# An opening list ordered anew, and U's first lower part taken by VectorE instead of a second sum on TensorE

## The chip, the cores and the metric

The kernel runs on one core of a Trainium2 chip. The metric is the device time of one execution in microseconds (us). Before the change three runs took 706.29, 706.46 and 708.8 us; the median is 706.46 us. The chance that a text gives to "the same" means within 0.5% of it.

## The reference, cut to what matters

An attention over 32 learned memory slots, 8 batches of 8 heads, feeds a gated feed-forward layer over 4608 tokens. All is float32.

```python
a = softmax(phi)                                    # over the 576 positions, per memory slot
k_m, v_m = a.T @ k, a.T @ v                         # 32 slots per head
attn = softmax(q @ k_m.T / 8) @ v_m                 # 576 x 64 per head
x = attn heads side by side                         # 4608 x 512
out = (1 / (1 + exp(-(x @ w_gate))) * (x @ w_val)) @ w_out      # d_ff 1536
```

## The kernel before, in words

The product attn @ v_m @ [w_gate, w_val] is never made by way of x. For a batch b and a slice f of 128 of the 1536 columns the kernel makes U = v_m @ [w_gate, w_val] first (32 slots of 8 heads = 256 rows), and then G = U^T @ attn^T. A float32 product of this weight would take TensorE several passes, so each operand is split in an upper part that is rounded to the one-pass type fp32r, and a lower part, which is the rest; G and O are then the sum of three one-pass products (upper by upper, upper by lower, lower by upper). The pieces before that (T, K, t, S, U) are plain float32.

The first 20 of the 32 steps (b, f) of the first half, some 180 us of the span, are written out by hand in one list, OPENING. Each entry is traced behind the entry before it on TensorE, VectorE, ScalarE and GpSimd (`queued`, `step`), so on every one of these engines the instructions stand in the list's order; loads stand in the list's order on SyncE's queue (`move`). After the list a loop, ordered by the scheduler, goes through the rest. The names in the list (b is the batch, c one of two cuts of the 576 positions, 256 and 320 wide):

| entry | engine | what |
|---|---|---|
| phi, kvt, kvm, q, gate, out, more | SyncE | loads; gate and out fetch words of the weights, 8 bytes a number |
| amax, aexp, Z | VectorE, ScalarE, VectorE | softmax over phi |
| T, A | TensorE, ScalarE | transpose of it (two of 512 columns, one of the tails), copy out of PSUM |
| K, B, t, V | TensorE, ScalarE, TensorE, ScalarE | k_m and v_m, scaled, transposed, kept as kT (V b 0) and vT (V b 1) |
| S, mx, ms, ex, nz, nm | TensorE, then VectorE but ex on ScalarE | scores and softmax; tp (batch 0) or tr and tn turn them |
| hi, lo | ScalarE, VectorE | upper and lower part of attn^T |
| sz, bt / ws, wb, wh, wl | ScalarE, VectorE / ScalarE and VectorE | words of w_gate, w_val / w_out made into float32 and split |
| U, uh, ul | TensorE, ScalarE, VectorE | U for two f at a time, its upper and lower part |
| G, sg, gm, gh, gl | TensorE, ScalarE, VectorE, ScalarE, VectorE | gate and value, sigmoid, product, its two parts |
| O, E, row | TensorE, ScalarE, SyncE | times w_out, copy out, store |
| W n | TensorE | n fillers: matmuls whose result nobody reads, to keep the engine running |

PSUM has eight banks; four rotate under the name pu_t, three of the acc banks join them until the first O.

One pair, (b 0, f 0 and 1), is in BY_PE: its lower part is not subtracted. `um 0 0` multiplies the upper part by a tile `minus` (the identity times -1) and adds U's eight products a second time in the same banks; what is left in PSUM is U minus its upper part, and ScalarE copies it (`u_rest`, L773). All other pairs go through `u_lo`, whose subtraction is `rest` (L246). `copy` (L230) goes to ScalarE or, with act=False, to VectorE.

Of the kernel before, what the change touches and what calls it, by code (L numbers as in the profile page):

```python
# [78 lines left out]
q 1 0; ex 0 0; mx 0 1; U 0 0; q 1 1; A 1 0; out 1; A 1 2; ms 0 1; uh 0 0; nz 0 0; ex 0 1; W 10;
um 0 0; nm 0 0; sz 3; nz 0 1; tp 0 0; nm 0 1; hi 0 0; W 7; ul 0 0; lo 0 0; K 1 0; tp 0 1; hi 0 1;  # L80
wb 0; G 0 0 0; sz 2; kvm 2 0; lo 0 1; amax 2; G 0 0 1; wh 0; aexp 2; G 0 1 0; bt 3; wl 0; K 1 1;
bt 2; sg 0 0 0; G 0 1 1; B 1; kvt 2; kvm 2 1; gm 0 0 0; sg 0 0 1; out 2; gh 0 0 0; gm 0 0 1; out 3;
sg 0 1 0; t 1; gl 0 0 0; T 2 1; gm 0 1 0; V 1 0; Z 2; T 2 2; sg 0 1 1; S 1 0; V 1 1; gm 0 1 1;
A 2 1; tr 1 0; S 1 1; gh 0 0 1; U 0 2; tr 1 1; A 2 2; T 2 0; uh 0 2; mx 1; U 1 0; A 2 0; ul 0 2;
gh 0 1 0; K 2 0; uh 1 0; ms 1; ws 1; ul 1 0; K 2 1; gl 0 0 1; ex 1; O 0 0 0; gl 0 1 0; wb 1; nz 1;
wh 1; more 0; G 0 2 1; kvt 3; B 2; phi 3; kvm 3 0; wl 1; O 0 0 1; nm 1; G 0 2 0; sg 0 2 0;
gh 0 1 1; G 0 3 0; sg 0 2 1; gm 0 2 0; ws 2; tn 1; O 0 1 0; gh 0 2 0; hi 1; G 0 3 1; gm 0 2 1;
gl 0 2 0; gl 0 1 1; gh 0 2 1; wb 2; sg 0 3 0; lo 1; t 2; sg 0 3 1; O 0 1 1; wh 2; gm 0 3 0; sz 4;
q 2 0; wl 2; q 2 1; G 1 0 0; gl 0 2 1; keep 0; ws 3; gm 0 3 1; amax 3; O 0 2 0; G 1 0 1; gh 0 3 0;
sg 1 0 0; gl 0 3 0; V 2 0; wb 3; gh 0 3 1; V 2 1; gm 1 0 0; more 1; sg 1 0 1; O 0 2 1; wh 3;  # L90
gm 1 0 1; wl 3; S 2 0; S 2 1; tr 2 0; aexp 3; O 0 3 0; tr 2 1; gl 0 3 1; mx 2; U 1 2; gh 1 0 0;
E 0 3 0 0; T 3 2; E 0 3 0 1; row 0 3 0; O 0 3 1; gl 1 0 0; uh 1 2; ms 2; row 0 3 1; G 1 1 0;
gh 1 0 1; ul 1 2; ex 2; O 1 0 0; gl 1 0 1; nz 2; G 1 1 1; sg 1 1 0; A 3 2; gm 1 1 0; E 0 3 1 0;
gh 1 1 0; T 3 0; row 0 3 2; sg 1 1 1; nm 2; G 1 2 0; kvm 3 1; E 0 3 1 1; keep 1; gm 1 1 1; O 1 0 1;
sg 1 2 0; tn 2; gh 1 1 1; G 1 2 1; gm 1 2 0; A 3 0; T 3 1; sg 1 2 1; G 1 3 0; gl 1 1 0; gh 1 2 0;
phi 4; gm 1 2 1; A 3 1; bt 4; hi 2; O 1 1 0; more 2; sz 5; lo 2; K 3 0; gl 1 1 1; q 3 0; gl 1 2 0;
U 2 0; q 3 1; sg 1 3 0; keep 2; gm 1 3 0; K 3 1; Z 3; O 1 1 1; B 3; amax 4; uh 2 0; G 1 3 1;
gh 1 2 1; ul 2 0; gh 1 3 0; O 1 2 0; bt 5; sg 1 3 1; sz 6; gm 1 3 1; G 2 0 0; more 3; gl 1 2 1;
row 0 3 3; gl 1 3 0; t 3; sg 2 0 0; G 2 0 1; V 3 0; gm 2 0 0; gh 1 3 1; V 3 1; gh 2 0 0; S 3 0;
sg 2 0 1; gm 2 0 1; O 1 2 1; tr 3 0; aexp 4; S 3 1; U 2 2; tr 3 1; gh 2 0 1; O 1 3 0; mx 3; uh 2 2;  # L100
G 2 1 0; E 1 3 0 0; ul 2 2; E 1 3 0 1; gl 1 3 1; O 1 3 1; row 1 3 1; ms 3; ws 4; G 2 1 1; gl 2 0 0;
ex 3; gl 2 0 1; nz 3; O 2 0 0; sg 2 1 0; E 1 3 1 0; G 2 2 0; gm 2 1 0; E 1 3 1 1; gh 2 1 0;
sg 2 1 1; O 2 0 1; sg 2 2 0; gm 2 1 1; row 1 3 0; gm 2 2 0; gh 2 1 1; G 2 2 1; gh 2 2 0; gl 2 2 0;
gl 2 1 0; bt 6; U 3 0; sg 2 2 1; gl 2 1 1; more 4; O 2 1 0; uh 3 0; row 1 3 2; gm 2 2 1; kvt 4;
nm 3; G 2 3 0; ul 3 0; O 2 1 1; sg 2 3 0; tn 3; gh 2 2 1; G 2 3 1; gm 2 3 0; hi 3; O 2 2 0; lo 3;
sg 2 3 1; again 0; sz 7; row 1 3 3; gl 2 2 1; G 3 0 0; gm 2 3 1; O 2 2 1; gh 2 3 0; sg 3 0 0;
gh 2 3 1; gm 3 0 0; G 3 0 1; wb 4; gl 2 3 0; more 5; O 2 3 0; sg 3 0 1; wh 4; gm 3 0 1; gl 2 3 1;
G 3 1 0; Z 4; E 2 3 0 0; wl 4; E 2 3 0 1; row 2 3 0; gh 3 0 0; T 4 1; row 2 3 1; sg 3 1 0;
gl 3 0 0; U 3 2; A 4 1; gm 3 1 0; G 3 1 1; uh 3 2; gh 3 0 1; ul 3 2; O 2 3 1; sg 3 1 1; gl 3 0 1;
bt 7; G 3 2 0; E 2 3 1 0; sg 3 2 0; E 2 3 1 1; gm 3 1 1; more 6; O 3 0 0; gh 3 1 0; G 3 2 1; ws 5;  # L110
O 3 0 1; gl 3 1 0; gm 3 2 0; sg 3 2 1; wb 5; gm 3 2 1; U 0 4; wh 5; row 2 3 2; keep 3; G 3 3 0;
uh 0 4; kvm 4 1; row 2 3 3; gh 3 1 1; ul 0 4; more 7; O 3 1 0; gh 3 2 0; gl 3 2 0; G 3 3 1;
gl 3 1 1; wl 5; sg 3 3 0; ws 6; O 3 1 1; sg 3 3 1; gh 3 2 1; gm 3 3 1; G 0 4 0; gm 3 3 0; gl 3 2 1;
O 3 2 0; sg 0 4 0; gh 3 3 0; gm 0 4 0; gl 3 3 0; wb 6; U 0 6; O 3 2 1; uh 0 6; wh 6; ul 0 6;
G 0 4 1; gh 3 3 1; O 3 3 0; sg 0 4 1; gh 0 4 0; gm 0 4 1; gl 3 3 1; E 3 3 0 0; E 3 3 0 1; gh 0 4 1;
G 0 5 0; gl 0 4 0; row 3 3 0; O 3 3 1; sg 0 5 0; row 3 3 1; gm 0 5 0; again 1; gl 0 4 1; gh 0 5 0;
wl 6; G 0 5 1; O 0 4 0; sg 0 5 1; E 3 3 1 0; gm 0 5 1; E 3 3 1 1; row 3 3 2; G 0 6 0; kvm 4 0;
more 8; row 3 3 3; O 0 4 1; sg 0 6 0; ws 7; gm 0 6 0; gl 0 5 0; G 0 6 1; gh 0 5 1; fetch 0 0; wb 7;
gh 0 6 0; gl 0 5 1; O 0 5 0; sg 0 6 1; gm 0 6 1; gl 0 6 0; G 0 7 0; sg 0 7 0; wh 7; gh 0 6 1; wl 7;
T 4 2; O 0 6 0; gm 0 7 0; gl 0 6 1; gh 0 7 0; A 4 2; gl 0 7 0; sz 8; fetch 0 1; T 4 0; O 0 7 0;  # L120
# [1482 lines left out]
```

## Time and profile before

| what | us |
|---|---|
| runs | 706.29, 706.46, 708.8 |
| the profiled execution's own time | 706.82 |
| its span, first to last instruction | 705.0 |
| TensorE busy | 697.7 |
| VectorE busy | 520.7 |
| ScalarE busy | 403.0 |
| GpSimd busy | 97.2 |

The span is what the rows of the profile add up to; 1.8 us of the execution lie outside it. A busy TensorE says little by itself, since fillers count as busy and a matmul's end is modelled: what it could have done without is found by looking at which matmuls stand in a stretch and how far apart they start.

### The profile page before, as it was taken

What the parts mean: (1) busy time and instruction counts of PE and PEld (TensorE: products, weight loads), DVE (VectorE), ACT (ScalarE), POOL (GpSimd) and SP (SyncE); (2) the same over time, 40 slices, a digit from 0 to 9 for tenths busy, and PEclk for the clock granted to TensorE, in tenths of its full rate; (3) what the DMA queues carried; (4) which work ended last, traced back from release to release, by engine and by line L of the source; (5) the groups of instructions that cost most, each with busy time, mean ns of one, the idle gap of its engine ahead of it and who ended that gap; (6) DMA issues with size and microseconds to landing.
All of it is one profiled execution on the core that took longest, in us unless ns stands there. A gap on an engine that the chain in (4) does not pass through costs nothing.

```text
span 705.0 us, 15881 instructions
## 1 busy us (share of the span) xinstructions
PE 697.7 (99%) x6295; PEld 621.3 (88%) x6295; DVE 520.7 (74%) x1086; ACT 403.0 (57%) x915; POOL 97.2 (14%) x135
## 2 busy tenths in 40 slices
...
GB/s 359 413 275 339 253 196 170 232 136 250 280 253 265 276 183 135 133 351 244 164 113 182 148 357 206 292 271 43 284 137 164 227 108 276 77 295 56 238 111 105
DMA packets 52298, 151.49 MB, mean 215 GB/s; under 512 B 5888, under 2 KB 24320, under 8 KB 50176
## 3 DMA queue, kind: packets, MB, share of 16 engines
...
## 4 chain that ended last, share of the span: by engine, by line
PE 98%; DMA 1%; DVE 1%; ACT 0%; issue 0%; DVEq 0%; POOL 0%; POOLq 0%; SPq 0%
PE pu_t L256 59%; PE acc L256 38%; DMA ph<-in_phiT_dram 1%; DVE row L1291 0%; ACT ph L224 0%; DVE nmx L430 0%; DVEq L1599 0%; DVE x L1291 0%; POOL ident masks.py:199 0%; POOL ident masks.py:197 0%; POOLq masks.py:199 0%; SPq L242 0%; DVEq L1291 0%; POOLq L1593 0%
## 5 line engine op out<-in xcount | busy, mean ns | idle before, releaser
L256 PE MATMUL pu_t<-at_hi,u_hi 128*128 128x256 f32 (+1 forms) x760 | 224.5, 295 | 0.0
L256 PE MATMUL pu_t<-at_hi,u_lo 128*128 128x256 f32 (+1 forms) x760 | 222.6, 293 | 0.0
L256 PE MATMUL pu_t<-at_lo,u_hi 128*128 128x256 f32 (+1 forms) x760 | 222.6, 293 | 0.0
L256 PEld LDWEIGHTS pu_t<-at_hi,u_hi 128*128 128x128 f32 x760 | 142.8, 188 | 4.3 <-issue 1.4
L256 PEld LDWEIGHTS pu_t<-at_lo,u_hi 128*128 128x128 f32 x760 | 142.7, 188 | 2.0
L256 PEld LDWEIGHTS pu_t<-at_hi,u_lo 128*128 128x128 f32 x760 | 142.6, 188 | 0.0
L246 DVE TENSOR_TENSOR g_lo<-x,g_hi 128x128 fp32r<-128x128 f32 (+2 forms) x193 | 88.5, 464 | 15.0 <-ACT g_hi L1103 13.8
L224 ACT ACTIVATE x<-pu_t 128x320 f32<-128x320 f32 (+1 forms) x128 | 52.2, 410 | 81.8 <-PE pu_t L256 81.0
L1053 DVE TENSOR_TENSOR x<-pu_t,x 128x320 f32<-128x320 f32 (+1 forms) x128 | 58.1, 455 | 47.2 <-ACT x L224 29.1
L256 PE MATMUL acc<-wo_hi,g 128*128 128x512 f32 x256 | 91.1, 400 | 0.0
L256 PE MATMUL acc<-wo_hi,g_hi 128*128 128x256 f32 x276 | 78.3, 284 | 0.0
L256 PE MATMUL acc<-wo_lo,g_hi 128*128 128x256 f32 x276 | 76.9, 278 | 0.0
L256 PE MATMUL acc<-wo_hi,g_lo 128*128 128x256 f32 x276 | 76.8, 278 | 0.0
L246 DVE TENSOR_TENSOR u_lo<-pu_t,u_hi 128x512 fp32r<-128x512 f32 x92 | 58.3, 682 | 13.9 <-ACT u_hi L230 13.9
L242 POOL DMA_DIRECT2D out_dram<-row x48 | 42.4, 966 | 145.1 <-DVE row L1197 132.4
L256 PEld LDWEIGHTS acc<-wo_hi,g 128*128 128x128 f32 x256 | 48.0, 188 | 15.3 <-issue 5.8
L256 PEld LDWEIGHTS acc<-wo_hi,g_hi 128*128 128x128 f32 x276 | 51.8, 188 | 10.1 <-issue 9.2
L256 PE MATMUL acc<-ring,g_hi 128*128 128x256 f32 x332 | 60.2, 281 | 0.0
L256 PEld LDWEIGHTS acc<-ring,g_hi 128*128 128x128 f32 x332 | 50.5, 188 | 9.2 <-issue 6.7
L1103 ACT CAST g_hi<-x 128x512 fp32r<-128x512 f32 x63 | 39.1, 620 | 30.9 <-DVE x L1101 30.9
L230 ACT CAST u_hi<-pu_t 128x512 fp32r<-128x512 f32 x92 | 49.0, 590 | 12.3 <-PE pu_t L256 7.8
L256 PEld LDWEIGHTS acc<-wo_hi,g_lo 128*128 128x128 f32 x276 | 51.8, 188 | 0.0
...
## 6 DMA issues: line engine op xcount, KB each, us to landing
...
words<-in_wgv_dram SPq DMA_DIRECT2D x5, 1023.6 KB, 7.5
...
```

Of the source, the lines that this page charges most:

```text
L224: last_act[0] = nc.scalar.activation(*args, **kw)
L230: (nc.scalar.copy if act != swapped[0] else nc.vector.tensor_copy)(to, x)
L242: last_move[queue] = queues[queue].dma_start(dst, src, **how)
L246: return nc.vector.tensor_tensor(lo, x, hi.bitcast(F32), op=ALU.subtract)
L256: last_pe[0] = do(*args, **kw)
L1053: last_prod[0] = nc.vector.tensor_tensor(x[:, :n], val, x[:, :n], op=ALU.mult)
L1103: nc.scalar.copy(gh[:, 2:6], x[:, 1:5])
```

## The change

It takes BY_PE, `u_minus`, `u_rest` and the tile `minus` away, so that `ul 0 0` is a VectorE subtraction like all others. The list holds the same entries otherwise, in another order, with fillers W of other number and at other places, and 44 entries bear a ' behind their name: their copies go to the other engine (22 gh', ten A', four V', three hi' and three uh' go from ScalarE to VectorE, two wh' the other way). `swapped` already was in the kernel and no entry used it.

```diff
-BY_PE = [(0, 0)]
 OPENING = """
-phi 0; gate 0; kvm 0 0; kvt 0; kvm 0 1; amax 0; aexp 0; W 24; T 0 0; T 0 2; T 0 1; A 0 2; A 0 0;
...
+W 4; W 4; W 6; W 2; phi 0; W 4; W 1; amax 0; aexp 0; T 0 1; Z 0; T 0 0; A' 0 0; W 2; W 5; T 0 2; kvt 0;
+kvm 0 0; kvm 0 1; A' 0 2; K 0 0; A 0 1; K 0 1; B 0; t 0; W 2; W 1; W 4; V 0 0; V' 0 1; q 0 0; q 0 1;
...
 """
...
-    def u_minus(b, fs):
-
-        pb, hi = loaded[b, "u", fs[0]], U[b, fs[0]][0]
-        for r in range(2):
-            matmul(pb[r], minus, hi[:, r, : len(fs)], start=True, stop=False)
-        u_sum(b, fs, pb, False)
-
-    def u_rest(b, fs):
-        pb, nf = loaded.pop((b, "u", fs[0])), len(fs)
-        hi, lo = U[b, fs[0]]
-        for r in range(2):
-            last_u[0] = nc.scalar.copy(lo[:, r, :nf], pb[r])
...
-    minus = pools["conv"].tile([P, P], F32R, name="minus", bufs=1)
-    nc.scalar.activation(minus, ident, AF.Copy, scale=-1.0)
...
-        "ul": lambda b, f: (u_rest if (b, f) in BY_PE else u_lo)(*pair(b, f)),
+        "ul": lambda b, f: u_lo(*pair(b, f)),
```

The fillers: before, 24 stand ahead of the list and 76 in it, all ahead of the first G; now 24 and 111, of which 104 ahead of the first G.

SyncE's queue, the first loads of the kernel before. wg_106 and wg_105 are the words of w_gate and w_val for f 0 and 1 (gate 0, gate 1).

```order
L242 DMA ph<-in_phiT_dram 128x1152
L242 DMA wg_106<-in_wgv_dram 128x8189
L242 DMA kvm_150<-in_kvm_dram 128x2048
L242 DMA kvt<-in_kvt_dram 128x512
L242 DMA kvm_154<-in_kvm_dram 128x2048
L242 DMA q<-in_qT_dram 128x1024
L242 DMA ph<-in_phiT_dram 128x1152
L242 DMA wg_105<-in_wgv_dram 128x8189
```

The same queue now; at_hi takes the third phi.

```order
L240 DMA ph<-in_phiT_dram 128x1152
L240 DMA kvt<-in_kvt_dram 128x512
L240 DMA kvm_200<-in_kvm_dram 128x2048
L240 DMA kvm_202<-in_kvm_dram 128x2048
L240 DMA q<-in_qT_dram 128x1024 x2
L240 DMA q<-in_qT_dram 128x256
L240 DMA ph<-in_phiT_dram 128x1152
L240 DMA wg_106<-in_wgv_dram 128x8189
L240 DMA at_hi<-in_phiT_dram 128x1152
L240 DMA wg_105<-in_wgv_dram 128x8189
```

The loads of batch 0 moved ahead of the weights' words, and the third phi moved ahead of the second of them.

ScalarE around U's first parts, before: acc_383 and acc_384 are U's two banks, e the scores of batch 0.

```order
L224 ACTIVATE e<-e 128x512
L230 COPY left<-pu_t 128x512
L230 COPY tails<-pu_t 64x128 x2
L230 CAST u_hi<-acc_383 128x512
L230 CAST u_hi<-acc_384 128x512
L224 ACTIVATE e<-e 128x640
L273 ACTIVATE wg_102<-wg_103,over 128x1024
L274 ACTIVATE wg_102<-wg_102,under 128x1024
L230 CAST at_hi<-acc_437 128x2x256
L773 CAST u_lo<-acc_383 128x512
L773 CAST u_lo<-acc_384 128x512
```

ScalarE now, from the second exponential of the scores (ex 0 1) to the first sigmoid; the words of f 0 (two pairs of 128x512) stand right ahead of it. wg_101 is the tile of f 0 and 1, acc_450 and acc_451 are U's banks, wo_raw takes words of w_out (ws 0).

```order
L222 ACTIVATE e<-e 128x640
L271 ACTIVATE wg_101<-wg_105,over 128x1024
L272 ACTIVATE wg_101<-wg_101,under 128x1024
L228 COPY left<-pu_t 128x512
L222 ACTIVATE at_hi,z<-at_hi,nmx 128x576 x2
L271 ACTIVATE wo_raw<-words,over 128x512
L272 ACTIVATE wo_raw<-wo_raw,under 128x512
L228 CAST at_hi<-acc_423 128x2x256
L228 CAST u_hi<-acc_450 128x512
L228 CAST u_hi<-acc_451 128x512
L222 ACT_TABLE_LOAD
L222 ACTIVATE sg<-acc_506 128x256
```

The words of f 0 and 1 moved behind the first exponential, the third softmax over phi (two exponentials of 128x576) and the words ws 0 moved to between the second one and U's upper part, and the two casts of U's lower part are gone.

VectorE at the same place, before: the first lower part of attn^T and what follows it.

```order
L246 TENSOR_TENSOR at_lo<-acc_437,at_hi 128x2x256
L356 SCALAR_TENSOR_TENSOR wo_raw<-words,wo_raw 128x512
L246 TENSOR_TENSOR at_lo<-pu_t,at_hi 128x2x256
L246 TENSOR_TENSOR at_lo<-pu_t,at_hi 128x2x64
L430 TENSOR_REDUCE nmx<-at_hi 128x2
L230 CAST wo_hi<-wo_raw 128x512
```

VectorE now.

```order
L244 TENSOR_TENSOR at_lo<-acc_423,at_hi 128x2x256
L244 TENSOR_TENSOR u_lo<-acc_450,u_hi 128x512
L244 TENSOR_TENSOR u_lo<-acc_451,u_hi 128x512
L228 CAST at_hi<-pu_t 128x2x256
L228 CAST at_hi<-pu_t 128x2x64
L354 SCALAR_TENSOR_TENSOR wo_raw<-words,wo_raw 128x512
L244 TENSOR_TENSOR at_lo<-pu_t,at_hi 128x2x256
L244 TENSOR_TENSOR at_lo<-pu_t,at_hi 128x2x64
```

U's two subtractions and the upper part of the second cut were added to VectorE ahead of the first G.

## Rows read from the trace of the kernel before

**Rows 1.** The page's head and its busy times.
```profile
span 705.0 us, 15881 instructions
PE 697.7 (99%) x6295; PEld 621.3 (88%) x6295; DVE 520.7 (74%) x1086; ACT 403.0 (57%) x915; POOL 97.2 (14%) x135
```

**Rows 2.** Stretches: length, then PE, PEld, DVE, ACT, POOL busy, clock, DMA share, GB/s.
```profile
0.00:20.00 20.00, 17.51 (x190) 14.10 (x191) 6.16 (x15) 11.94 (x25) 0.70 (x6) 1.00 0.92 364
20.00:80.00 60.00, 59.97 (x663) 49.26 (x661) 50.66 (x89) 54.23 (x103) 0.00 (x0) 1.00 0.82 307
80.00:180.00 100.00, 100.00 (x847) 82.38 (x846) 57.93 (x109) 63.60 (x131) 0.21 (x1) 1.00 0.58 210
```

**Rows 3.** Timeline of TensorE: start, length, instruction, count, [idle before, releaser].
```profile
1.37 7.46 PE L256 MATMUL acc<-ident 128*128 128x256 bf16 x48 [1.37 <-POOL ident masks.py:199]
8.66 1.15 PE L256 MATMUL pu_t<-ident,ph 128*128 128x128 f32 x9
...
13.07 1.08 PE L256 MATMUL pu_t<-kvm,e 128*32 128x128 f32 x32 [0.42 <-DMA kvm<-in_kvm_dram]
...
14.30 0.83 PE L256 MATMUL acc<-ident 128*128 128x256 bf16 x6
...
16.49 2.00 PE L256 MATMUL acc<-kT,q 128*128 128x64 f32 x16 [0.18 <-ACT kT L230]
...
19.34 1.69 PE L256 MATMUL acc<-ident 128*128 128x256 bf16 x14
20.86 2.48 PE L256 MATMUL pu_t<-kT,q 128*128 128x64 f32 x32
23.27 0.66 PE L256 MATMUL pu_t<-ident,ph 128*128 128x128 f32 x4
23.86 1.09 PE L256 MATMUL acc<-wg,vT 64*32 64x512 f32 x16
...
26.12 0.98 PE L256 MATMUL acc<-u_hi,minus 128*128 128x512 f32 x2
...
28.05 0.66 PE L256 MATMUL acc<-ident,e 128*128 128x128 f32 x4
...
31.15 0.36 PE L256 MATMUL pu_t<-at_hi,u_hi 128*128 128x256 f32 x1
...
35.85 0.28 PE L256 MATMUL acc<-at_hi,u_lo 128*128 128x256 f32 x1
36.06 1.08 PE L256 MATMUL pu_t<-kvm,left 128*32 128x128 f32 x32
...
43.12 1.09 PE L256 MATMUL acc<-wg,vT 64*32 64x512 f32 x16
```

**Rows 4.** Size of one load of a step's words, from the DMA view.
```profile
wg<-in_wgv_dram SPq DMA_DIRECT2D x4, 1023.6 KB, 10.8
```

**Rows 5.** Timeline of ScalarE, same columns as TensorE's.
```profile
19.36 1.23 ACT L273 ACTIVATE wg<-wg,over 128x1024 f32<-128x1024 int8 x1 [0.29 <-DMA wg<-in_wgv_dram]
20.63 1.45 ACT L274 ACTIVATE wg<-wg,under 128x1024 int16<-128x1024 f32 x1
...
22.40 0.78 ACT L273 ACTIVATE wo_raw<-words,over 128x512 f32<-128x512 int8 x1
23.21 0.88 ACT L274 ACTIVATE wo_raw<-wo_raw,under 128x512 int16<-128x512 f32 x1
...
30.16 1.06 ACT L773 CAST u_lo<-acc 128x512 fp32r<-128x512 f32 x2
```

**Rows 6.** VectorE and ScalarE by shape: busy us, mean ns of one, idle before.
```profile
L246 DVE TENSOR_TENSOR u_lo<-pu_t,u_hi 128x512 fp32r<-128x512 f32 x92 | 58.3, 682 | 13.9 <-ACT u_hi L230 13.9
L230 DVE CAST wo_hi<-wo_raw 128x512 fp32r<-128x512 f32 x8 | 3.3, 412 | 0.0
L230 ACT CAST g<-sg 128x256 fp32r<-128x256 f32 x64 | 25.9, 405 | 14.0 <-DVE sg L841 12.5 <-DVE wo_lo L246 1.5
```

More of the change, by code (lines that the diff above doesn't have):

```diff
@@ L72 @@
 FIRST_U = [(0, [0, 1]), (0, [2, 3]), (1, [0, 1]), (1, [2, 3]), (2, [0, 1]), (2, [2, 3]), (3, [0, 1]), (3, [2, 3]), (0, [4, 5]), (0, [6, 7]), (1, [4, 5]), (1, [6, 7])]
-BY_PE = [(0, 0)]
 OPENING = """
-phi 0; gate 0; kvm 0 0; kvt 0; kvm 0 1; amax 0; aexp 0; W 24; T 0 0; T 0 2; T 0 1; A 0 2; A 0 0;
-q 0 0; phi 1; A 0 1; W 5; K 0 0; gate 1; sz 0 1; q 0 1; out 0; gate 3; sz 0 0; W 6; K 0 1; kvm 1 0;
-Z 0; B 0; kvt 1; amax 1; gate 2; phi 2; W 6; t 0; kvm 1 1; V 0 0; bt 0 1; aexp 1; W 4; S 0 0;
-bt 0 0; V 0 1; Z 1; T 1 1; mx 0 0; T 1 2; sz 1; ms 0 0; W 14; A 1 1; ws 0; bt 1; S 0 1; T 1 0;
@@ L79 @@
[L79 to L120, printed above, removed]
@@ L121 @@
-E 0 7 0 0; G 0 7 1; A 4 0; row 0 7 0; sg 0 7 1; O 0 5 1; O 0 6 1; E 0 7 0 1; row 0 7 1; U 1 4;
-gm 0 7 1; uh 1 4; K 4 0; gh 0 7 1; ul 1 4; fetch 0 2; gl 0 7 1; K 4 1; U 1 6; B 4; bt 8; uh 1 6;
-O 0 7 1; t 4; V 4 0; fetch 0 3; V 4 1; E 0 7 1 0; ul 1 6; row 0 7 2; E 0 7 1 1; row 0 7 3;
+W 4; W 4; W 6; W 2; phi 0; W 4; W 1; amax 0; aexp 0; T 0 1; Z 0; T 0 0; A' 0 0; W 2; W 5; T 0 2; kvt 0;
+kvm 0 0; kvm 0 1; A' 0 2; K 0 0; A 0 1; K 0 1; B 0; t 0; W 2; W 1; W 4; V 0 0; V' 0 1; q 0 0; q 0 1;
+S 0 0; phi 1; amax 1; S 0 1; aexp 1; mx 0 0; ms 0 0; mx 0 1; Z 1; ms 0 1; W 1; W 2; T 1 0; T 1 1; T 1 2;
@@ new lines @@
+ex 0 0; A' 1 2; W 6; W 20; W 5; W 5; W 4; gate 0; sz 0 1; A' 1 0; phi 2; nz 0 0; amax 2; nm 0 0; bt 0 1;
+gate 1; sz 0 0; ex 0 1; sz 1; bt 1; bt 0 0; A 1 1; aexp 2; out 0; kvt 1; ws 0; kvm 1 0; W 10; W 3;
+tp 0 0; hi 0 0; nz 0 1; nm 0 1; lo 0 0; W 6; W 7; U 0 0; kvm 1 1; uh 0 0; ul 0 0; K 1 0; T 2 1; tp 0 1;
+hi' 0 1; wb 0; lo 0 1; G 0 1 0; T 2 2; sg 0 1 0; gm 0 1 0; wh 0; gh' 0 1 0; gl 0 1 0; gate 2; K 1 1;
+A' 2 2; sz 2; bt 2; W 6; G 0 0 0; W 1; A' 2 1; B 1; t 1; G 0 0 1; T 2 0; sg 0 0 0; wl 0; gm 0 0 0;
@@ new lines @@
+gate 3; sz 3; V' 1 0; V 1 1; sg 0 0 1; gh' 0 0 0; A 2 0; q 1 0; q 1 1; bt 3; S 1 0; tr 1 0; S 1 1; U 0 2;
+G 0 1 1; gm 0 0 1; tr 1 1; gh' 0 0 1; uh 0 2; ul 0 2; Z 2; gl 0 0 0; mx 1; ms 1; sg 0 1 1; G 0 2 1;
+G 0 3 0; kvm 2 0; out 1; kvt 2; K 2 0; kvm 2 1; out 3; kvm 3 0; out 2; phi 3; kvm 3 1; ws 1; sg 0 2 1;
+ex 1; gm 0 2 1; gm 0 1 1; wb 1; wh' 1; nz 1; gl 0 0 1; U 1 0; gh 0 1 1; uh 1 0; sg 0 3 0; ul 1 0;
+gl 0 1 1; nm 1; gm 0 3 0; wl 1; tn 1; gh 0 2 1; hi' 1; K 2 1; B 2; O 0 0 0; O 0 0 1; G 0 2 0; t 2; V 2 0;
@@ new lines @@
+gh 0 3 0; V 2 1; G 0 3 1; sg 0 3 1; ws 2; gm 0 3 1; wb 2; U 1 2; O 0 1 0; uh 1 2; O 0 1 1; lo 1; G 1 0 0;
+gl 0 3 0; wh' 2; gh 0 3 1; wl 2; gl 0 3 1; gl 0 2 1; O 0 2 1; sg 1 0 0; ul 1 2; sg 0 2 0; gm 0 2 0;
+gm 1 0 0; gh 0 2 0; ws 3; G 1 0 1; sg 1 0 1; gl 0 2 0; O 0 2 0; amax 3; wb 3; keep 0; kvt 3; q 2 0;
+q 2 1; S 2 1; S 2 0; gm 1 0 1; wh 3; wl 3; O 0 3 0; gh' 1 0 0; aexp 3; E 0 3 0 0; row 0 3 0; G 1 2 1;
+G 1 1 0; O 0 3 1; sg 1 2 1; tr 2 1; tr 2 0; mx 2; ms 2; ex 2; G 1 1 1; G 1 2 0; sg 1 1 0; E 0 3 0 1;
@@ new lines @@
+more 0; row 0 3 1; more 1; sz 4; gm 1 2 1; gl 1 0 0; O 1 0 0; nz 2; G 1 3 0; T 3 0; nm 2; gm 1 1 0;
+gh' 1 1 0; gl 1 1 0; gh' 1 0 1; gl 1 0 1; O 1 1 0; T 3 2; sg 1 1 1; sg 1 2 0; gm 1 1 1; gh' 1 1 1;
+E 0 3 1 1; sg 1 3 0; E 0 3 1 0; gl 1 1 1; gm 1 2 0; A 3 0; gh 1 2 0; tn 2; A' 3 2; sz 5; T 3 1; O 1 0 1;
+O 1 1 1; G 1 3 1; A' 3 1; gh 1 2 1; hi 2; sg 1 3 1; U 2 0; gm 1 3 0; gl 1 2 0; bt 4; more 2; phi 4;
+K 3 0; O 1 2 0; U 2 2; K 3 1; uh 2 0; lo 2; ul 2 0; G 2 0 0; gm 1 3 1; Z 3; sz 6; B 3; gh 1 3 1;
@@ new lines @@
+gh' 1 3 0; uh' 2 2; ul 2 2; gl 1 3 1; t 3; G 2 0 1; gl 1 3 0; gl 1 2 1; O 1 3 0; sg 2 0 0; sg 2 0 1;
+V' 3 0; gm 2 0 0; amax 4; gm 2 0 1; gh' 2 0 1; V 3 1; q 3 0; S 3 0; q 3 1; S 3 1; O 1 2 1; G 2 1 0;
+tr 3 0; tr 3 1; gh' 2 0 0; aexp 4; bt 6; mx 3; sg 2 1 0; O 1 3 1; E 1 3 1 0; row 0 3 3; row 0 3 2;
+keep 1; row 1 3 2; again 0; keep 2; gm 2 1 0; ms 3; ex 3; gh' 2 1 0; gl 2 0 0; gl 2 1 0; gl 2 0 1; nz 3;
+G 2 1 1; sg 2 1 1; gm 2 1 1; G 2 3 0; G 2 2 0; sg 2 2 0; gm 2 2 0; gh 2 2 0; E 1 3 0 1; nm 3; tn 3;
@@ new lines @@
+row 1 3 1; G 2 2 1; sg 2 2 1; G 2 3 1; O 2 0 0; O 2 1 0; O 2 0 1; gh' 2 1 1; gl 2 1 1; E 1 3 0 0;
+O 2 1 1; U 3 2; U 3 0; E 1 3 1 1; hi' 3; sg 2 3 0; gl 2 2 0; gm 2 3 0; bt 5; kvm 4 1; more 3; more 4;
+kvm 4 0; row 1 3 0; row 1 3 3; sg 2 3 1; gm 2 2 1; ws 4; gh' 2 2 1; gm 2 3 1; gl 2 2 1; gh 2 3 0;
+gh 2 3 1; lo 3; keep 3; uh 3 2; O 2 2 1; O 2 2 0; uh' 3 0; ul 3 0; G 3 0 0; G 3 0 1; sg 3 0 0; sz 7;
+gl 2 3 0; ul 3 2; bt 7; wb 4; more 5; more 6; O 2 3 0; sg 3 0 1; E 2 3 0 0; row 2 3 0; G 3 2 1; G 3 1 0;
@@ new lines @@
+gm 3 0 0; sg 3 2 1; sg 3 1 0; gh' 3 0 0; Z 4; gm 3 0 1; wh 4; gl 2 3 1; E 2 3 0 1; gh' 3 0 1; O 2 3 1;
+row 2 3 1; gl 3 0 0; G 3 1 1; O 3 0 0; gm 3 1 0; gm 3 2 1; gh' 3 1 0; gl 3 1 0; E 2 3 1 1; U 0 4;
+uh' 0 4; ul 0 4; O 3 1 0; G 3 3 1; G 0 5 0; G 3 2 0; G 0 4 1; gh 3 2 1; sg 3 1 1; wl 4; gm 3 1 1;
+gh' 3 1 1; sg 3 3 1; sg 0 5 0; sg 0 4 1; E 2 3 1 0; gl 3 1 1; gm 3 3 1; gh' 3 3 1; T 4 1; A 4 1;
+gl 3 0 1; gl 3 2 1; gm 0 5 0; ws 5; gl 3 3 1; sg 3 2 0; gh' 0 5 0; G 0 4 0; sg 0 4 0; wb 5; wh 5;
+gm 3 2 0; gh 3 2 0; O 3 0 1; O 3 1 1; O 3 2 1; O 3 3 1; wl 5; gl 0 5 0; T 4 0; G 3 3 0; sg 3 3 0; A' 4 0;
```

13 lines of the change are left out of this document (10 added, 3 removed).

## The prediction

> **What bounds the kernel now.** I read the page's busy times first: TensorE 697.7 of a span of 705.0 us, VectorE 520.7, ScalarE 403.0 [rows 1]. Fillers count as busy, so I went on to the table by stretch: from 20 to 80 us TensorE is busy 59.97 of 60, from 80 to 180 us 100.00 of 100, at the full granted clock [rows 2]. The third view is TensorE's timeline up to 36 us: there the reader sees which starts lie apart by more than the work of the piece before. The list's first product G starts at 31.15 [rows 3]. Behind it the three products of 256 columns start 0.11 apart, and I find no gap that a piece's own pace doesn't account for until the list ends near 180 us. So behind 31.15 the list's work is fixed, TensorE does it without a pause, and nothing can be won there. All that can be won lies ahead of 31.15.
>
> What fills the time from the first transpose (8.66) to the first G (31.15) [rows 3], 22.5 us? A row runs into the next by about 0.17 (the 14 fillers at 19.34 are 1.69 long, and the next starts 1.52 later), so I count from start to start:
> - the list's own pieces, some 12.4: the first nine transposes 0.98, the three K at 1.23 each (13.07 to 14.30), S 1.83 and 2.41 (20.86 to 23.27), U's first sum 1.0, and the other transposes at 0.11 each, 2.4 for 22 of them;
> - 52 of the 100 fillers, at 1.52 / 14 = 0.109 each: 5.7;
> - the second sum, from 26.12 to 28.05: 1.93;
> - what is left, 2.5, is waiting.
>
> **The change, part by part.** *The second sum.* TensorE loses 1.93 us of work. ScalarE loses the two casts of it, 1.06 [rows 5]; VectorE gains two subtractions from PSUM at 0.682 [rows 6], 1.36. They stand between U's upper part and the first G, so they are paid on the path, less what the third product of G doesn't need yet.
>
> *Fillers.* 100 become 135 (the numbers of both lists are in the text on the change): 35 x 0.109 = 3.8 us. A filler runs whether or not anybody waits; it is free only where TensorE would have waited anyway. There were 2.5 us of such waits. So if every wait went, the whole is -1.9 + 3.8 - 2.5 = -0.6 us; that is the floor, and no order of the other engines gets below it.
>
> *The loads.* Batch 0 passes ahead of the 1 MB of words of gate 0 [rows 4]. At the 364 GB/s of the first 20 us [rows 2] 1 MB takes 2.9 us, so kvm, for which K waited until 13.07 [rows 3], lands at some 10.2, and TensorE's own order then lets K 0 1 start at 11.5, S 0 0 at 14.9 instead of 16.49, S 0 1 end at 19.1 instead of 23.27. What is late next: the words. Gate 0 lands at some 17.3 and gate 1 at 21.2; before, gate 1 was there at 19.36 (the row's releaser [rows 5]). The third phi now goes ahead of it.
>
> *ScalarE's chain to the first G.* This sets the start of G now. S 0 0 done at 16.7 and VectorE's maximum and subtraction behind it (0.7 each, as the nearest row of 128x512 from PSUM) put the first exponential at 18.3. Behind it ScalarE has, in its order: that exponential 0.5; words of f 0, two pairs of 128x512 at the 0.78 + 0.88 of such a pair [rows 5], less overlap 3.2; the second exponential 0.65; words of f 1, 1.23 + 1.45 [rows 5], 2.6 net; one A copy 0.5; two exponentials of phi 1.6; words ws 0, 1.6; upper part of attn^T 0.5; upper part of U, like the two casts of 1.06 [rows 5]. Sum 12.3, so 30.6. The lower part follows on VectorE, 0.682 behind the first of U's banks. That allows the first G at 31.3. TensorE's own way there: S 0 1 done at 19.1, transposes to 20.4, 53 fillers 5.8, four transposes 0.5, 13 fillers 1.4, so U 0 0 at 28.1, 1.0, then K 1 0 1.23 and nine transposes 1.0: 31.3 too. The two meet, and the first G stands at 31.3 against 31.15 [rows 3].
>
> At 31.3 one transpose piece more is done than before (0.44), and 7 of the 35 extra fillers (0.76) stand behind it. Walking on with the same durations, I find two short waits: t 1 for B 1 (0.5, behind the words of f 2 on ScalarE) and U 0 2 for its words (0.25). G 0 1 1 then ends at 43.7; before, the list had done as much at 43.12 [rows 3]. So +0.6. Further on I find no wait of TensorE, but VectorE is only 0.2 to 1 us ahead at several places; I add 0.2 for that.
>
> *More switches.* Where plain float32 follows on the one-pass products, the start comes later: 35.85 to 36.06 is 0.21 for a piece that takes 0.11 [rows 3]. Such places, both ways, are 37 behind the first G before and 46 now. At between 0 and 0.1 each, nine cost 0 to 0.9; I take the middle, 0.4.
>
> *The 44 copies.* They cost TensorE nothing as long as VectorE keeps up; it is hidden by 9.3 us of idle time from 20 to 80 us and 42 from 80 to 180 [rows 2]. The 22 gh' are casts of 128x256 in SBUF, for which VectorE has no row: between half of the 128x512 cast, 0.21, and all of it, 0.41; ScalarE took 0.405 [rows 6]. I take 0.3. If the cover goes, each is paid in full.
>
> The 128x512 cast from SBUF took VectorE 0.412, the subtraction of the same width that reads PSUM 0.682 [rows 6]. The Trainium skill ("VectorE: DVE Perf Modes", section "Mode 2×_2P — use both read ports for one tensor") says that a copy with one source gives two results a cycle, float32 too, if source and target are in SBUF, and that PSUM doesn't allow it. The rows agree in size. By it 256 columns would be about 0.28, an estimate, so the gh' are the cheap ones of the 44, and the A' and V', which read PSUM, speak against the change: they take VectorE longer than they took ScalarE.
>
> **The sum.** The span is 705.0 + 0.6 + 0.4 + 0.2 = 706.2, with the 1.8 outside it 708.0. The profiled execution, 706.82, was 0.36 above the median of 706.46; so 707.7 for the median.
>
> **Rivals.**
> *All waits go (A).* If words and casts come earlier than I reckon, the fillers cover every wait: -0.6, 705.9. That is 1.2 below the walk's +0.6 and without its 0.6 for switches and VectorE. For it: my walk leaves only 0.75 of wait behind the first G, both short. Against it: the DMA engines are 0.92 busy in the first 20 us [rows 2], so the landings that hold TensorE ahead of S 0 0 hardly come earlier, and the switches cost at least something in the one place that I show.
>
> *VectorE becomes the bound between 20 and 80 us (B; ends slower).* It was busy 50.66 of the 60 [rows 2]. Added there: U's lower part 1.4, three copies of 128x512 from PSUM 2.0 (by the 0.682 of the subtraction [rows 6]), five of 128 columns 1.4 (at 0.28, between a quarter of the 0.682 and all of it), one V' 0.4, four gh' 1.2, one upper part of 1152 columns 0.8 (0.412 x 2.25 at most), less two casts of w_out 0.82 [rows 6]: net 6.4, so 57 of 60. Nothing of it fails if it stands where VectorE was idle; but most of its 9.3 us of idle time are waits for ScalarE and TensorE, which a new order needn't keep apart. In place of the 0.2 that I allow: if half of the 6.4 falls where TensorE waits for VectorE, the time is 707.5 + 3.2 = 710.7; if all of it, 713.9. It decides for slower from 2.5 us on. Against it: my walk, in which it stays ahead, if narrowly.
>
> *The clock falls (C).* Every stretch shows the full granted clock [rows 2], but the first 48 fillers took from 1.37 to 8.66, 7.3 us, and at 0.109 each they would be 5.2 [rows 3]: a start at the lower level cost 2.0. A pause of TensorE ahead of the first G long enough to bring it back would cost about that on top of itself, 710. The Trainium skill ("TensorE: Matmul & The Clock Gate", section "What's actually happening") says that the throttled level (1.2 GHz) is the default and that activity releases the full one (2.4 GHz); those first rows agree with it. Against: no pause of TensorE in my walk is longer than 1 us, and the 53 fillers stand where the longest would be.
>
> *The change does not do what it says*: the second sum leaves, but no wait goes and fillers and sum cancel: -1.9 + 3.8 = +1.9 less nothing, 708.4, which the measurement calls the same.
>
> **How the numbers follow.** Within 0.5%, 3.5 us, a measurement can't tell this kernel from itself; the bounds are 702.9 and 710.0. My forecast, 707.7 with 705.9 to 709.2, has a chance of 0.68; A 0.10; no wait goes 0.08; B 0.11, of which a third stays under 710; C 0.03. Faster by over 0.5% lies 3.0 us below a floor made of counts and rows: 0.02, for an error in it. Slower: two thirds of B, C, and the upper end of the forecast's own errors, 0.11. The same: 0.87. The range goes from the floor with the 0.2 of the runs' spread below it, 705.7, to 2.8 us of B's 6.4, 710.3.
>
> **What would show it.** In the profile of the changed kernel: no matmul of u_hi by minus; first transpose at about 8.3, S 0 1 done near 19, a row of over 50 fillers behind it; ScalarE without a pause from 18.3 to 30.6; the first G at 31.3; and the second G of f 1 done at 43.7. VectorE busy some 57 of 60 from 20 to 80, TensorE with no idle time over 0.3 there. I am wrong if the first G starts before 30.4 or after 32.5, if TensorE's starts show waits for VectorE behind it (B), if a stretch shows a granted clock below 1.00 behind the start (C), or if the loop behind 180 us takes another time than before.

## The result: slower, and the profile after

The changed kernel takes 712.23 us (median of six runs, 711.04 to 714.39), the kernel before 706.44; the ratio is 1.0078, 95% interval 1.0061 to 1.0094. A second set of runs on another occasion gives 711.45 and 1.0080 (1.0054 to 1.0105). By the two ratios that is some 5.6 us more; the forecast was 1.2 more, and the measured time lies above its range.

The changed kernel's profiled execution took 714.18 us, the longer end of its runs. Its page begins so, against [rows 1]:

```profile
span 712.4 us, 15911 instructions
PE 700.8 (98%) x6312; PEld 624.3 (88%) x6312; DVE 539.8 (76%) x1148; ACT 386.9 (54%) x856; POOL 96.9 (14%) x135
```

The table by stretch, columns as in [rows 2]:

```profile
20.00:80.00 60.00, 58.08 (x641) 48.29 (x640) 54.60 (x102) 50.02 (x80) 0.00 (x0) 1.00 0.76 287
80.00:180.00 100.00, 98.82 (x843) 80.89 (x842) 68.83 (x149) 56.55 (x104) 0.07 (x1) 1.00 0.61 212
180.00:330.00 150.00, 148.38 (x1081) 127.04 (x1080) 115.76 (x228) 77.01 (x174) 27.51 (x33) 1.00 0.71 238
```

Before, the first two stretches had TensorE busy 59.97 and 100.00 [rows 2]. The third, the loop's beginning, was this in the kernel before:

```profile
180.00:330.00 150.00, 149.97 (x1118) 130.16 (x1117) 118.79 (x234) 80.08 (x182) 29.06 (x35) 1.00 0.72 242
```

TensorE lost 1.9, 1.2 and 1.6 us, 4.7 in all; 0.3 of it lies ahead of the first G, the rest behind it. The granted clock is 1.00 in every stretch.

How much of that belongs to the list shows where the loop behind it begins. Its first product in the kernel before, in the changed kernel, and in the changed kernel with both repairs that are tried below (e15):

```profile
180.04 0.37 PE L256 MATMUL pu_t<-at_hi,u_hi 128*128 128x256 f32 x1
```

```profile
185.19 0.28 PE L254 MATMUL pu_t<-at_hi,u_hi 128*128 128x256 f32 x1
```

```profile
183.88 0.28 PE L254 MATMUL pu_t<-at_hi,u_hi 128*128 128x256 f32 x1
```

From the first G to there the list took 148.9 us before, 153.7 now and 151.4 in e15; from there to the end of the span the loop took 525.0, 527.2 and 523.5. So both parts of the kernel lost time, the loop too, which the change doesn't edit.

Ahead of the first G it went nearly as the walk had it. TensorE's timeline of the changed kernel, against [rows 3]:

```profile
7.92 1.04 PE L254 MATMUL pu_t<-ident,ph 128*128 128x128 f32 x8
...
10.87 1.06 PE L254 MATMUL pu_t<-kvm,e 128*32 128x128 f32 x32
...
18.62 0.50 PE L254 MATMUL acc<-ident 128*128 128x256 bf16 x3
...
20.13 5.95 PE L254 MATMUL acc<-ident 128*128 128x256 bf16 x53
...
28.27 1.09 PE L254 MATMUL acc<-wg,vT 64*32 64x512 f32 x16 [0.34 <-DVE wg L354]
...
31.48 0.37 PE L254 MATMUL acc<-at_hi,u_hi 128*128 128x256 f32 x1
```

Batch 0's scores are done at 18.6 (19.1 was reckoned), the row of 53 fillers stands behind them, and the first G starts at 31.48 (31.3). Then come the waits. What TensorE waited for in the changed kernel from 31 to 200 us (sum, times, longest); the same question of the kernel before has no answer, not one row:

```profile
PE pu_t L254 <- ACT sg L222: 1.9, 2, 1.3
PE pu_t L254 <- DMA q<-in_qT_dram: 1.2, 1, 1.2
PE pu_t L254 <- DVE wg L354: 0.4, 1, 0.4
PE pu_t L254 <- DVE sg L824: 0.4, 1, 0.4
PE acc L254 <- ACT row L872: 0.2, 1, 0.2
```

A view of waits counts from the modelled end of the matmul before, some 0.17 too late, so each costs that much more than its row says.

The largest stands at 198 us, in the loop, 13 us behind the end of the list. ScalarE of the changed kernel there, and the matmul that waited:

```profile
191.09 0.75 ACT L271 ACTIVATE kvm<-words,over 128x512 f32<-128x512 int8 x1
196.19 0.33 ACTq L240 DMA_DIRECT2D left<-part  x1
196.56 0.41 ACT L228 CAST g<-sg 128x256 fp32r<-128x256 f32 x1 [4.71 <-DMA row<-part]
196.87 0.86 ACT L272 ACTIVATE kvm<-kvm,under 128x512 int16<-128x512 f32 x1
197.60 0.41 ACT L222 ACTIVATE sg<-pu_t 128x320 f32<-128x320 f32 x1
```

```profile
198.06 0.41 PE L254 MATMUL pu_t<-at_hi,u_hi 128*128 128x320 f32 x1 [1.27 <-ACT sg L222]
```

ScalarE issues the load of a partial row (left<-part) itself. By the profile's releaser that issue waits until an earlier load, row<-part, has landed, and everything behind it stands still for 4.7 us, the sigmoid for which TensorE waits included. In the kernel before ScalarE stood in the same way (there the row names a store, out_dram<-left, as what was waited for):

```profile
185.27 0.76 ACT L273 ACTIVATE kvm<-words,over 128x512 f32<-128x512 int8 x1
189.49 0.33 ACTq L242 DMA_DIRECT2D left<-part  x1
189.92 0.44 ACT L224 ACTIVATE sg<-pu_t 128x320 f32<-128x320 f32 x1 [3.89 <-DMA out_dram<-left]
```

There, 3.9 us cost TensorE nothing: it had other work at that point. One difference is when these loads are issued. The first of them, before and now:

```profile
175.28 0.33 ACTq L242 DMA_DIRECT2D row<-part  x1
```

```profile
187.96 0.98 ACTq L240 DMA_DIRECT2D row<-part  x2
```

Before, the first stood 4.8 us ahead of the loop's first product, and the issue that held ScalarE 9.4 behind it; now they stand 2.8 and 11.0 behind it. What in the new list makes them later was not tried. The other sigmoid, near 140 us, waited behind a copy that needs a row buffer whose store has not landed. ScalarE of the changed kernel, and the matmul:

```profile
139.43 0.59 ACT L872 COPY row<-acc 128x512 f32<-128x512 f32 x1 [4.71 <-DMA part<-row]
139.91 0.41 ACT L228 CAST g<-sg 128x256 fp32r<-128x256 f32 x1
140.21 0.25 ACT L228 COPY left<-sg 128x64 f32<-128x64 f32 x1
140.36 0.44 ACT L222 ACTIVATE sg<-pu_t 128x320 f32<-128x320 f32 x1
```

```profile
140.85 0.42 PE L254 MATMUL pu_t<-at_hi,u_hi 128*128 128x320 f32 x1 [0.59 <-ACT sg L222]
```

### The profile page after: what moved, and what is told of

It is laid out like the page before. It is cut to its first block, busy times and chain, and to the rows that moved or that the text cites. A ratio compares the mean times of both kernels' runs of the same rounds, so it can differ in the third digit from the quotient of the medians.

```text
span 712.4 us, 15911 instructions
## 1 busy us (share of the span) xinstructions
PE 700.8 (98%) x6312; PEld 624.3 (88%) x6312; DVE 539.8 (76%) x1148; ACT 386.9 (54%) x856; POOL 96.9 (14%) x135
## 4 chain that ended last, share of the span: by engine, by line
PE 86%; DMA 5%; ACT 4%; DVE 3%; issue 2%; DVEq 0%; POOL 0%; ACTq 0%; POOLq 0%; SPq 0%
PE pu_t L254 53%; PE acc L254 33%; DMA part<-row 2%; ACT wg L272 1%; DMA row<-part 1%; DMA q<-in_qT_dram 1%; ACT wg L271 1%; DMA ph<-in_phiT_dram 1%; DVE wg L354 1%; DVE row L1274 0%; ACT g L228 0%; DVE sg L824 0%; ACT sg L222 0%; ACT kvm L272 0%; ACT ph L222 0%
## 5 line engine op out<-in xcount | busy, mean ns | idle before, releaser
L254 PE MATMUL acc<-wo_hi,g 128*128 128x512 f32 x256 | 89.2, 400 | 0.2 <-ACT row L872 0.2
L254 PE MATMUL pu_t<-wg,vT 64*32 64x512 f32 x752 | 51.2, 599 | 0.7 <-DVE wg L354 0.4
```

The source lines that it names most:

```text
L254: last_pe[0] = do(*args, **kw)
```

## The experiments

Each ratio is to the kernel before, with its 95% interval; the changed kernel has 1.0078 (1.0061 to 1.0094).

**Only the second sum gone, in the old order** (e1).

```diff
-BY_PE = [(0, 0)]
+BY_PE = []
-um 0 0; nm 0 0; sz 3; nz 0 1; tp 0 0; nm 0 1; hi 0 0; W 7; ul 0 0; lo 0 0; K 1 0; tp 0 1; hi 0 1;
+nm 0 0; sz 3; nz 0 1; tp 0 0; nm 0 1; hi 0 0; W 7; ul 0 0; lo 0 0; K 1 0; tp 0 1; hi 0 1;
```

> The list of before, with U's first lower part subtracted by VectorE and the second sum gone; nothing else changed. Theory 1 (the first G is bound by what VectorE and ScalarE hand over, so TensorE's 1.93 us turn into a wait): first G's products run from about 31.2 as before, time 706.4, within 0.5 of before. Theory 2 (TensorE's own work bounds the stretch): 1.9 less, 704.5. Theory 3 (two more subtractions of 0.68 on VectorE ahead of G): up to 1.4 more, 707.8.

706.52 us, ratio 1.0000 (0.9984 to 1.0016): theory 1. The first G starts at 30.85, and its second product waits until 31.84 for the lower part of attn^T from VectorE. The part of the change that it is named after is worth nothing by itself, within 1.1 us.

**Fewer fillers in the new order** (e3), **more in the old** (e8).

```diff
-ex 0 0; A' 1 2; W 6; W 20; W 5; W 5; W 4; gate 0; sz 0 1;
+ex 0 0; A' 1 2; W 5; gate 0; sz 0 1;
```

> The changed kernel with 35 of the 53 fillers behind the third transpose taken out. Theory 1 (ScalarE's chain to U's upper part sets the first G): first G stays at 31.2 to 31.5, TensorE waits about 3.8 us there, time 712, within 0.7. Theory 2 (the fillers themselves are what it costs): 3.8 less, 708.4. Theory 3 (the wait lets the clock fall): a granted clock under 1.00 behind it and up to 2 more, 714.

```diff
-sz 1; ms 0 0; W 14; A 1 1;
+sz 1; ms 0 0; W 14; W 35; A 1 1;
```

> The kernel of before with 35 fillers added behind its 14, ahead of S 0 1. Theory 1 (a filler costs its 0.109 where nobody waits, and before had at most some waits ahead of the first G): 3.8 less the waits that it covers, 1.5 to 3.8 more, 708 to 710.3. Theory 2 (they run while TensorE would have waited): no change, 706.5.

Without 35 fillers the changed kernel takes 711.77, 1.0070 (1.0047 to 1.0093); the first G starts at 31.41, and TensorE stands idle where the fillers were. Its timeline:

```profile
25.55 0.63 PE L254 MATMUL acc<-ident,e 128*128 128x128 f32 x4 [2.40 <-DVE e L668]
26.02 1.58 PE L254 MATMUL acc<-ident 128*128 128x256 bf16 x13
...
31.41 0.37 PE L254 MATMUL acc<-at_hi,u_hi 128*128 128x256 f32 x1
```

With 35 more, the old order takes 709.75, 1.0050 (1.0033 to 1.0067), 3.4 of the 3.8 that they last. So a filler's price is that of the place: 0.1 where TensorE goes through, nothing that the times resolve where VectorE and ScalarE are late anyway. The extra fillers are not what the change costs. In e3's profiled execution the clock did not fall behind that pause of 2.4 us, it is 1.00 from 24 to 32; in that of e18, below, it did.

**Only the 44 copies, in the old order** (e10), **and its two halves** (e13, e14). The list of before with a ' behind the same 44 names, then behind the 22 gh alone, then behind the other 22; two places of e10:

```diff
-W 24; T 0 0; T 0 2; T 0 1; A 0 2; A 0 0;
+W 24; T 0 0; T 0 2; T 0 1; A' 0 2; A' 0 0;
...
-bt 0 0; V 0 1; Z 1; T 1 1;
+bt 0 0; V' 0 1; Z 1; T 1 1;
```

> The kernel of before with its own order, second sum and fillers; only the 44 copies go to the other engine (22 gh, ten A, four V, three hi, three uh from ScalarE to VectorE, two wh the other way). Theory 1 (the copies fill VectorE, which hands over late): 2 to 6 more, 708.5 to 712.5, with waits for VectorE on TensorE. Theory 2 (the new order makes the loss, copies are hidden): within 0.7 of 706.4.

> The kernel of before; of the 44 copies only the 22 gh (128x256, SBUF to SBUF, 0.28 each on VectorE) go to VectorE. Theory 1 (the waits behind 100 us in the run with all copies, for g, sg and at_lo, come from them): 2.5 to 3.5 more, 709 to 710, nothing lost before 100 us. Theory 2 (they are short and hidden, the copies out of PSUM make the loss): within 0.7 of 706.4.

> The kernel of before; the other 22 copies change engine (ten A, four V, three hi, three uh to VectorE, two wh to ScalarE). Theory 1 (the waits up to 46 us in the run with all copies come from these, the later ones from gh): 2.5 to 3.5 more, 709 to 710, all of it ahead of 100 us. Theory 2 (these make the whole loss): 712 to 713.

All 44: 713.38, 1.0086 (1.0064 to 1.0107). The 22 gh: 708.74, 1.0016 (0.9999 to 1.0032), hardly to be told from none, and TensorE has no wait from 26 to 260 us; theory 1 falls, theory 2 is the nearer. The other 22: 711.20, 1.0055 (1.0040 to 1.0069). What TensorE waited for in e10, from 26 to 260 us:

```profile
PE acc L256 <- DVE tails L230: 1.3, 1, 1.3
PE acc L256 <- DVE g L246: 0.9, 1, 0.9
PE pu_t L256 <- DVE sg L841: 0.8, 2, 0.5
PE acc L256 <- DVE at_lo L246: 0.7, 1, 0.7
PE pu_t L256 <- DVE at_lo L246: 0.6, 1, 0.6
PE acc L256 <- DVE e L670: 0.4, 1, 0.4
```

All of it is VectorE. In the run of the 22 others the same places wait, those behind 100 us too, which I had put down to gh: both theories of e14 fall in part. In the old order the copies alone cost as much as the change does, 6.1 us against 5.6, but by other waits: not one of these is for ScalarE.

**Some copies taken back in the new order** (e17): all ten A' and four V', one place of it here.

```diff
-T 0 0; A' 0 0; W 2; W 5; T 0 2;
+T 0 0; A 0 0; W 2; W 5; T 0 2;
```

> The changed kernel with the ten A and four V copies (PSUM to SBUF) back on ScalarE. Theory 1 (in the changed order too the copies on VectorE make the loss; these 14 are about half of their time): 1.5 to 3 less, 709 to 710.7. Theory 2 (the changed order is made for them, ScalarE then hands over late): 712 or more.

717.59, 1.0155 (1.0136 to 1.0175): theory 2, and 5 us worse than the changed kernel. Its waits, the first three from 26 to 260 us:

```profile
PE pu_t L254 <- ACT sg L222: 3.5, 4, 1.0
PE acc L254 <- ACT at_hi L222: 2.0, 1, 2.0
PE pu_t L254 <- ACT left L499: 1.8, 1, 1.8
```

So order and copies can't be priced apart. The old order with the copies waits for VectorE, the new order with fewer of them for ScalarE. All gh taken back in the new order was not tried.

**What holds ScalarE** (e5, e6, e15, and e16 on the kernel before). The loads of partial rows go to SyncE's queue (with them the last two stores of output rows, which the same queue had); the copy E 2 3 1 1 goes behind the sigmoid; both; and the first on the kernel before.

```diff
-    queues = {"batch": nc.sync, "stream": nc.gpsimd, "rows": nc.scalar}
+    queues = {"batch": nc.sync, "stream": nc.gpsimd, "rows": nc.sync}
```

```diff
-gl 3 1 0; E 2 3 1 1; U 0 4;
+gl 3 1 0; U 0 4;
...
-gh 3 2 1; sg 3 1 1; wl 4;
+gh 3 2 1; sg 3 1 1; E 2 3 1 1; wl 4;
```

> The changed kernel with the loads of partial rows, which ScalarE's own queue issues (row<-part, left<-part), issued from SyncE's queue. Theory 1 (an issue that waits on ScalarE's queue holds the sigmoid behind it, and TensorE waits 1.3 for that near 198 us): that wait goes, 1 to 1.5 less, 710.7 to 711.2. Theory 2 (the same wait holds SyncE's loads instead): 712 or more, a new wait for a load.

> The changed kernel with one copy out of PSUM (E 2 3 1 1, which ScalarE can start only when a store of a row before has landed) put behind the two casts and the sigmoid that follow it. Theory 1 (ScalarE's 4.7 us wait for that store makes TensorE wait 0.6 near 140 us): that wait goes, 0.6 less, 711.6. Theory 2 (the store holds the bank that TensorE needs next): no change.

> The changed kernel with both edits to what holds ScalarE: the loads of partial rows on SyncE's queue, and the copy E 2 3 1 1 behind the sigmoid. Theory 1 (two separate hand-overs, each with its price): 2.5 to 3.5 less than the changed kernel, 708.5 to 709.5, ratio to before 1.003 to 1.004; no wait for a sigmoid on TensorE behind 130 us. Theory 2 (both are one and the same delay): like the loads alone, 1.004 or more.

> The kernel of before with the loads of partial rows issued from SyncE's queue instead of ScalarE's. Theory 1 (before, ScalarE also stood 3.9 us behind such a load near 186 us but TensorE had room, so only the changed kernel gains by this): within 0.5 of 706.4. Theory 2 (ScalarE's queue costs every such kernel): 1 to 3 less, 703.5 to 705.5.

The loads alone: 709.36, 1.0040 (1.0025 to 1.0054), clear of the changed kernel's interval, and more than the 1 to 1.5 us that theory 1 allowed. The copy alone: 711.51, 1.0063 (1.0043 to 1.0083), not clear of it, but in its profile the wait near 140 us is gone and the one near 196 stands. Both: 708.69, 1.0033 (1.0020 to 1.0046); its waits from 31 to 230 us have no sigmoid left:

```profile
PE pu_t L254 <- DVE sg L824: 0.4, 1, 0.4
PE pu_t L254 <- DVE wg L354: 0.3, 1, 0.3
PE acc L254 <- ACT row L872: 0.2, 1, 0.2
```

On the kernel before, the same edit of the queue gives 706.11, 0.9990 (0.9979 to 1.0001): nothing. The wait on ScalarE's queue was there all along; only the changed kernel pays for it. In e5 the wait near 140 us is gone as well (in that execution the copy waited 2.26 us for its store, not 4.71), so whether the two prices add up is not settled by the times (1.0040 and 1.0033 overlap). The loop's length fits: from its first product to the end of the span it takes 523.5 to 524.8 us in the profiles of e5, e15 and e18, with these loads on SyncE's queue, 525.7 to 527.2 in the three of the changed order with them on ScalarE's (the changed kernel, e6, e20), and 523.8 to 525.0 in five of the old order (before, e1, e8, e12, e16).

**Both, and fewer fillers** (e18), with the fillers of e3: 709.08, 1.0033 (1.0018 to 1.0049).

> As the run with both edits, and 35 of the 53 fillers taken out as well. Theory 1 (ScalarE and VectorE set the first G whatever TensorE does): within 0.5 us of the run with both edits. Theory 2 (with ScalarE no longer held, the fillers show): up to 3.8 less than it.

The times bear theory 1 out: with ScalarE no longer held the fillers have no price either. But the profiled execution shows what they cover. The 13 fillers behind the pause of 2.4 us, and the row of its table by stretch:

```profile
26.06 2.98 PE L254 MATMUL acc<-ident 128*128 128x256 bf16 x13
```

```profile
26.00:28.00 2.00, 2.00 (x12) 1.39 (x10) 2.00 (x3) 2.00 (x6) 0.00 (x0) 0.50 1.03 426
```

They took 2.98 where e3's took 1.58, at a granted clock of 0.50, the lower of the two levels, and the first G starts at 32.29. In e16's profile, behind a pause of 2.08 us for ScalarE's phi, the clock is 0.50 from 21 to 23 us as well. So such a pause can bring the clock down in one execution and not in another, and what the 53 fillers are worth as a guard against that is not settled.

**The late q** (e4), **and the changed kernel once more** (e20).

```diff
-q 2 1; S 2 1; S 2 0; gm 1 0 1;
+q 2 1; gm 1 0 1;
...
-row 0 3 0; G 1 2 1;
+row 0 3 0; G 1 2 1; S 2 1; S 2 0;
```

> The changed kernel with batch 2's scores (S 2 1 and S 2 0) two pieces of O and one of G later on TensorE, so that their load of q, which landed 1.2 us late, is no longer waited for. Theory 1 (the loss is a sum of late hand-overs, this one 1.4 us): 1.4 less, 710.8, no wait for q in the profile. Theory 2 (VectorE is behind as a whole, so that the wait comes back at the next piece): within 0.5 of 712.2.

> The changed kernel once more, unchanged, beside the two others. Theory 1 (the late q of batch 2 is a landing that varies from run to run; the waits for sg near 140 and 198 us are in the order and come back): ratio to before 1.006 to 1.009, sg waits again, the wait for q not in every profile. Theory 2: all its waits are the same again, q too.

The scores later: 715.27, 1.0122 (1.0094 to 1.0150), 3 us worse than unchanged. The wait for q is gone, and from 69 to 85 us TensorE waits five times, for VectorE's wo_hi, wo_lo, e and sg and for a row copy of ScalarE: what follows from the scores came later as well. Both theories had it no slower; they fall. The changed kernel's second profile (e20, from 31 to 230 us) has no wait for q either, but the sigmoids again:

```profile
PE pu_t L254 <- ACT sg L222: 1.8, 2, 1.1
PE pu_t L254 <- DVE sg L824: 0.6, 2, 0.4
PE pu_t L254 <- DVE wg L354: 0.3, 1, 0.3
```

So the 1.2 us for q belong to one execution, and the waits for sg to the order.

**An earlier first G** (e12): e1 with hi 0 0, ul 0 0 and lo 0 0 ahead of the second cut's work, G 0 0 0 and G 0 1 0 ahead of its turning (tp 0 1), and seven fillers less.

```diff
-sz 3; nz 0 1; tp 0 0; nm 0 1; hi 0 0; W 7; ul 0 0; lo 0 0; K 1 0; tp 0 1; hi 0 1;
+tp 0 0; hi 0 0; ul 0 0; lo 0 0; nz 0 1; sz 3; nm 0 1; K 1 0; G 0 0 0; G 0 1 0; tp 0 1; hi 0 1;
```

> The kernel of before without the second sum (as in the run of the sum alone), and with the order around the first G changed: hi 0 0, ul 0 0 and lo 0 0 ahead of the second cut's sum on VectorE and of the words of f 3 on ScalarE, G 0 0 0 and G 0 1 0 ahead of tp 0 1 and the upper part of the second cut, seven fillers less. Theory 1 (the 1.93 us were lost in the wait for the upper and lower part of attn^T, which now come 2 us sooner): first G at 28.5 to 29.2, 1.9 to 2.6 less than before, 703.9 to 704.5. Theory 2 (the second cut is then late and G 0 0 1 waits as long): within 0.5 of 706.4.

The first G starts at 28.88, 2.3 us earlier, and the time is 707.87, 1.0021 (1.0003 to 1.0039): all given back and a little more; neither theory had that. Its profile has two waits, 1.9 for a load of kvm up to 34.5 us and 1.2 for a copy of ScalarE up to 39.8. No run is faster than the kernel before beyond its interval.

## Why the prediction was wrong

*The second sum and the fillers.* Right in their sum, not one by one. The sum's 1.93 us were not to be had (e1), and the 35 fillers cost nothing in the new order (e3, e18), where I had booked -1.9, +3.8 and -2.5. The walk's first G at 31.3 stands against 31.48 in the profile; it varies by execution, from 31.18 (e5) to 32.45 (e15) in profiles of the new opening. The 53 fillers did fill a pause that VectorE sets.

*ScalarE's chain* took 12.1 us against the 12.3 of the sum, but ended at 31.45, not 30.6: two exponentials of phi 1 (from 17.84 to 19.38) stand ahead of the first one of the scores, and the chain had left them out.

*Up to the end of G 0 1 1.* 43.7 was reckoned, 44.5 it was: U 0 0 and U 0 2 waited 0.34 and 0.37 for VectorE's words. Here the sum itself slipped. From 31.15 to 43.12 are 11.97 us; 31.3 and 11.97, less 0.44, with 0.76 and the two waits of 0.75, is 44.3. So the walk should have given +1.2 for this stretch and not +0.6; +1.4 was measured.

*The step that failed* is "Further on I find no wait of TensorE, but VectorE is only 0.2 to 1 us ahead at several places; I add 0.2 for that", and with it that the loop would take the time that it took before, which the prediction had among its signs of being wrong. The walk moved ScalarE from instruction to instruction by durations alone. Two kinds of its instructions don't run by their duration: a copy into a row buffer, which waits for the store of the row before, and the issue of a load on its own queue, which waits for an earlier transfer. Both held the sigmoids behind them for 4.7 us. Taking both away gives back 3.3 us of the 5.6 (e15, by the ratios 1.0080 and 1.0033 of the same occasion), and leaves 2.3, by e15's interval 1.4 to 3.2, against the 1.2 of the forecast; 0.6 of that difference of 1.1 is the slip in the sum. The rest is not shown piece by piece. In e15's profile the list still takes 2.5 us more than before from the first G to the loop, where 1.05 was booked (0.6 less the 0.15 of the first G, and 0.4 and 0.2), with VectorE's waits of 0.3 and 0.4 behind 31 us and one of 0.2 for a row copy in it.

*The copies.* "They cost TensorE nothing as long as VectorE keeps up": it keeps up in the new order nearly everywhere (rival B's 20 to 80 us have VectorE 54.60 busy, not 57, and TensorE waits for it there 0.34 ahead of the first G and 0.37 behind). That the room that they took had covered late hand-overs is likely, but not shown. In the old order they cost 6.1 us by themselves, and every wait of TensorE behind 26 us is for VectorE there, which is rival B's mechanism in another kernel. The gh are the cheap ones, as reckoned. They take VectorE 287 ns each:

```profile
L228 DVE CAST g<-sg 128x256 fp32r<-128x256 f32 x22 | 6.3, 287 | 9.6 <-PE acc L254 9.2
```

The Trainium skill ("VectorE: DVE Perf Modes", section "Mode 2×_2P — use both read ports for one tensor") has two results a cycle for a copy with one source in SBUF; the estimate of 0.28 that the prediction worked out by it agrees with the trace's 0.287.

*The rivals.* A is out, since waits came. B is not what happened, though its end was on the right side. C is out for the profiled executions of the changed kernel: every stretch has the clock at 1.00. It was no empty rival, as e18's profile shows; its own first row, a start at the lower level, is read from the pace of the fillers alone, for the granted clock of 0 to 20 us is 1.00 in [rows 2]. That no wait goes and the fillers are paid in full (708.4) is out too, since they have no price here. That a full TensorE has no reserve for late hand-overs elsewhere, so that a third mechanism could make it slower, had no chance of its own: the 0.11 for slower came from B, C and the forecast's own errors, and that it pointed the right way in part was luck.
